# The two halves of a column group on rows of their own in the closing of a decode block: four vector operations over 64 columns and a store of 16 rows

## The chip, the cores and the metric

One core of one Trainium2 chip. The metric is device time in microseconds of one execution; lower is better. The span is the time from the first to the last instruction of one profiled execution, and all positions in the text (226.41 and the like) are microseconds from its start.

## What is computed

One decode step of a transformer block for two sequences (B = 2, one token each, D = 512), all in float32. Six modulation vectors come from `silu(c) @ w_mod`; then an attention over the last 4096 positions of a cache, then a feed-forward part, each gated:

```python
mod = (_silu(c) @ w_mod).reshape(c.shape[0], 6, 1, -1)
sa, ca, ga, sb, cb, gb = (mod[:, i] for i in range(6))
h = _layernorm(x) * (1 + ca) + sa
x = x + ga * attention(h, k_cache, v_cache, wq, wo)      # 32 heads, 8 key heads, last 4096 of 32768
h = _layernorm(x) * (1 + cb) + sb
x = x + gb * (_silu(h @ w1) @ w2)                          # w1 512 x 1792, w2 1792 x 512
```

The change is in the last line: the product with w2, the gate gb, the sum with x (called x1 in the kernel) and the store of the result, 2 x 512 numbers.

## The kernel before, in words

Nearly all of the time goes into reading weights and caches, 97.5 MB. Every load is issued by SyncE, in order, into a ring of eight slots of 16 KB a partition (`stream`, L70); a load starts when the slot's last reader is done. The order is w_mod, wq, eight pairs of key and value blocks, wo in two loads, w1 in two, and w2 in four: its 128-row tiles 0 to 7, 8 to 10, 11 and 12, and 13 (L599).

Two sequences fill only 2 of 128 partitions, so the kernel keeps a vector of 512 as four column groups of 128, and each group on its own 32 partitions: partition 32g + 16b holds columns 128g to 128g + 127 of sequence b. This is the layout of x1, of gb (a part of `mod_sp`) and of the result. Products use TensorE as four tiles side by side, each with weights of 128 x 32, whose column 16b holds sequence b; such a product fills the 32 rows of one group. A product in float32 is two instructions.

The tail, in order (names as in the trace):
- `busy(3)` (L641): products into `junk` whose result nobody reads.
- x1 is finished early, at L643, though it stands behind the junk products in the code. The hidden vector is turned, scaled and put through SiLU; `uT` (L657) holds it as 14 tiles of 128 x 32 weights, column 16b for sequence b.
- `yw` (L661): tiles 0 to 7 of w2, 512 columns each, spread over the four row groups; each row group so holds a part of the sum over all 512 columns.
- `y` (L671): tiles 8 to 10, one product of 128 columns for each column group g, into rows 32g.
- `gather` (L546): ScalarE and then VectorE copy the halves of yw to SBUF (L549, L550), and four products with `id4` (L552) add the four row groups up and put each column group on its rows, added to y.
- `yl` (L686): tiles 11 to 13, each column group in two halves of 64 columns, the halves in two banks of PSUM.
- The closing, on VectorE: y times gb (L694) plus x1 (L695), 128 columns each; then for each half, yl times gb (L699), and for each half the sum of both (L702).
- The store (L704): one DMA by SyncE, 8 rows of 128 numbers, from partitions 32g + 16b.

`inorder` keeps the instructions of one engine that are wrapped in it in the order of the code; the others are placed by the framework's scheduler where their data allow. The matmuls and the vector operations of the tail are wrapped, the copies by ScalarE and GpSimd's operations are not. `const` makes a tile for the whole kernel; tiles of one `tag` in the pool `once` share one place, and a new one waits for the last reader of the one before. Lines are those of the kernel before. The functions that the change touches:

Of the kernel before, what the change touches and what calls it, by code (L numbers as in the profile page):

```python
# [8 lines left out]
F32 = mybir.dt.float32  # L9
# [4 lines left out]
P = 128  # L14
B, D = 2, 512
# [8 lines left out]
def adaln_block(  # L24
# [19 lines left out]
    nc = tc.nc  # L44
# [7 lines left out]
    id4 = head.tile([P, 32], F32, name="id4")  # L52
    ring = ctx.enter_context(tc.tile_pool(name="ring", bufs=1))
    consts = ctx.enter_context(tc.tile_pool(name="consts", bufs=1))
    ktp = ctx.enter_context(tc.tile_pool(name="ktp", bufs=4))
    work = ctx.enter_context(tc.tile_pool(name="work", bufs=2))
    once = ctx.enter_context(tc.tile_pool(name="once", bufs=1))
# [3 lines left out]
    def const(shape, name):  # L61
        return consts.tile(shape, F32, name=name)

    def bank(tag, name):
        return (psum1 if tag in "CO" else psum).tile([P, 512], F32, tag=tag, name=name)
# [36 lines left out]
    rows8 = lambda t: t.rearrange("(ab r) m -> ab r m", r=16)[:, 0, :]  # L102
# [10 lines left out]
    ident = const([P, P], "ident")  # L113
# [98 lines left out]

    oTn = const([P, 32, 32], "oTn")
    nc.gpsimd.memset(oTn, 0.0)
    mod_a = const([P, 2, P], "mod_a")
    mod_sp = const([P, 4, P], "mod_sp")
    x1 = const([P, P], "x1")

    def silu_exp(t, name, shape):

        e = once.tile(shape, F32, tag="silu", name=name)
        nc.vector.tensor_scalar(e, t, -1.0, 87.0, op0=ALU.mult, op1=ALU.min)
        nc.scalar.activation(e, e, AF.Exp)
        nc.vector.tensor_scalar(e, e, 1.0, None, op0=ALU.add)
        nc.vector.reciprocal(e, e)
        return e
# [26 lines left out]
    def turned(t, name):  # L253
        o = const([P, 4, 32], name)
        nc.vector.transpose(o, t.rearrange("p (m k) -> p k m", k=4))  # L255
        return o
# [7 lines left out]
    for k in range(4):  # L264
        ab = wm[:, k, : 2 * D].rearrange("p (s g m) -> p g s m", s=2, g=4)
        cd = wm[:, k, 2 * D :].rearrange("p (s g m) -> p g s m", s=4, g=4)
        for g in range(4):
            r = slice(32 * g, 32 * g + 32)
            nc.tensor.matmul(m_a[r, :], scT[:, k, :], ab[:, g], start=(k == 0), stop=(k == 3))  # L269
        for g in range(4):  # L270
            r = slice(32 * g, 32 * g + 32)
# [11 lines left out]
    nc.vector.tensor_mul(h_a, xn, mod_a[:, 1, :])  # L283
    nc.vector.tensor_add(h_a, h_a, mod_a[:, 0, :])
    hq_T = turned(h_a, "hq_T")
    nc.scalar.copy(mod_sp.rearrange("p s m -> p (s m)"), m_sp)
    nc.gpsimd.tensor_scalar(mod_sp[:, 2, :], mod_sp[:, 2, :], 1.0, None, op0=ALU.add)
    ga, sb, cb1, gb = (mod_sp[:, s, :] for s in range(4))


    hT, uT = const([P, 4, 32], "hT_b"), const([P, F // P, 32], "uT")
    nc.gpsimd.memset(hT, 0.0)
    nc.gpsimd.memset(uT, 0.0)

    q_ps = [bank("D", f"q{n}") for n in range(2)]
    for n in range(2):
        for k in range(4):
            wv = wqt[:, k, :].rearrange("p (n s g m) -> p n g s m", n=2, s=4, g=G)  # L300
            for g in range(G):
# [4 lines left out]
                    start=(k == 0),  # L306
                    stop=(k == 3),
                )

    inorder = tc.keep_in_program_order  # L310
# [193 lines left out]
    ax = once.tile([P, P], F32, tag="ax", name="ax")  # L504
# [17 lines left out]
    for r in (0, 64):  # L522
# [4 lines left out]
            start=True,  # L527
            stop=True,
# [17 lines left out]
    def gather(acc, wide, name, start, stop):  # L546

        sb_ = once.tile([P, D], F32, tag="wide", name=name)
        nc.scalar.copy(sb_[:, : D // 2], wide[:, : D // 2])  # L549
        inorder(nc.vector.tensor_copy(sb_[:, D // 2 :], wide[:, D // 2 :]))  # L550
        for g in range(4):
            inorder(nc.tensor.matmul(  # L552
                acc[32 * g : 32 * g + 32, :],
                id4,
                sb_[:, g * P : (g + 1) * P],
                start=start,
                stop=stop,
            ))
# [15 lines left out]
    acc = bank("D", "acc_o")  # L574
    ao = bank("A", "ao")[:, :P]
    busy(6)
    for q in range(28):
        g = q % 4
# [4 lines left out]
            start=(q < 4),  # L583
            stop=(q >= 24),
        ))
    for q in range(28, 32):
        for g in range(4):
# [4 lines left out]
                start=(q == 28),  # L592
                stop=False,
# [3 lines left out]
    T2, WIDE = F // P, 8  # L597
    w2t = {}
# [26 lines left out]
    for k in range(4):  # L625
        for g in range(4):
# [4 lines left out]
                start=(k == 0),  # L631
                stop=(k == 3),
# [13 lines left out]
    z = once.tile([P, T2, B], F32, tag="z", name="z")  # L646
    for b in range(B):
        nc.vector.scalar_tensor_tensor(
            z[:, :, b],
            hidT[:, :, 16 * b],  # L650
            rstd[:, b : b + 1],
            hidT[:, :, 16 * b + 1],
            op0=ALU.mult,
            op1=ALU.add,
        )
    sg = silu_exp(z, "sgh", [P, T2, B])
    nc.vector.tensor_mul(uT[:, :, 0:32:16], z, sg)  # L657
    yw = bank("D", "acc_yw")
    for tt in range(WIDE):
        g = tt % 4  # L660
# [4 lines left out]
            start=(tt < 4),  # L665
            stop=(tt >= WIDE - 4),
        ))
    y = bank("D", "acc_y")[:, :P]
    for tt in range(WIDE, 11):
        for g in range(4):  # L670
            inorder(nc.tensor.matmul(  # L671
                y[32 * g : 32 * g + 32, :],
                uT[:, tt, :],
                w2t[tt][:, g * P : (g + 1) * P],
                start=(tt == WIDE),
                stop=False,
            ))
    gather(y, yw, "acc_y_sb", False, True)

    H = P // 2  # L680
    yl = [bank("A", f"acc_l{h}")[:, :H] for h in range(2)]
    for tt in range(11, T2):
        for h in range(2):
            for g in range(4):
                lo = g * P + h * H
                inorder(nc.tensor.matmul(  # L686
                    yl[h][32 * g : 32 * g + 32, :],
                    uT[:, tt, :],
                    w2t[tt][:, lo : lo + H],
                    start=(tt == 11),  # L690
                    stop=(tt == T2 - 1),
                ))
    yp = once.tile([P, P], F32, tag="xp", name="yp")
    inorder(nc.vector.tensor_mul(yp, y, gb))  # L694
    inorder(nc.vector.tensor_add(yp, yp, x1))  # L695
    yo = once.tile([P, P], F32, tag="yo", name="yo")
    for h in range(2):
        r = slice(h * H, (h + 1) * H)
        inorder(nc.vector.tensor_mul(yo[:, r], yl[h], gb[:, r]))  # L699
    for h in range(2):  # L700
        r = slice(h * H, (h + 1) * H)
        inorder(nc.vector.tensor_add(yo[:, r], yo[:, r], yp[:, r]))  # L702
    of = out.rearrange("b s d -> (b s) d")
    nc.sync.dma_start(of.rearrange("b (g m) -> g b m", m=P), rows8(yo))  # L704


_INS = ["A_x", "A_k_cache", "A_v_cache", "A_wq", "A_wo", "B_w1", "B_w2", "c", "w_mod"]
# [24 lines left out]
```

## Time and profile before

| | us |
|---|---|
| median of 3 runs | 235.51 |
| lowest and highest of them | 235.45, 235.78 |
| span of the profiled execution | 233.7 |
| TensorE, busy | 161.1 (69% of the span) |
| VectorE, busy | 115.6 (49%) |
| ScalarE, busy | 28.5 (12%) |
| GpSimd, busy | 10.5 (4%) |

Of the profiled execution the span is recorded, and no time of its own besides; the difference between the span and the lowest run, about 1.8 us, is what lies around it. An engine's busy time is an average over stages that wait for different things; for a change in the last 8 us, the rows of those 8 us decide.

### The profile page before, as it was taken

Reading aid. Unit: us, or ns where it says so; the run is one execution under the profiler, and the core shown is the slowest. Engines: PE = TensorE matmul, PEld = TensorE weight load, DVE = VectorE, ACT = ScalarE, POOL = GpSimd, SP = SyncE. Lnnn points to the kernel's source line nnn. Section 1 sums busy time; section 2 is a strip of 40 time slices with the busy share of each in tenths; the row PEclk is TensorE's granted clock in tenths of the full one; section 3 lists DMA queues with packets and bytes.
Section 4 is the critical chain, followed back from the end, with each engine's and each line's share of the span. In section 5 each row is a group of like instructions: output and inputs, shape, how many; then the busy total and the mean of one; then the engine's idle time right before and its main releaser. Section 6 shows DMA issues by size and latency. Waiting matters only on the chain.

```text
span 233.7 us, 2571 instructions
## 1 busy us (share of the span) xinstructions
PE 161.1 (69%) x1070; PEld 43.3 (19%) x1070; DVE 115.6 (49%) x179; ACT 28.5 (12%) x64; POOL 10.5 (4%) x35
## 2 busy tenths in 40 slices
PE   0004916859577839797598749759759779789684
PEld 0001401201111111211120201202112122324222
DVE  0007240278894758695197089259559540101232
ACT  2000210000311120120210201111020120102020
POOL 2004710000000000000000000000000000000000
PEclk9999985979999977999979999988997997999999
DMA  7998998999999999999999999999999999989991
GB/s 269 446 542 359 404 494 359 446 444 421 415 421 449 446 437 415 426 426 446 449 437 409 418 437 449 449 421 412 426 444 449 443 421 437 463 367 437 424 404 57
DMA packets 3794, 97.68 MB, mean 418 GB/s; under 512 B 432, under 2 KB 456, under 8 KB 968
## 3 DMA queue, kind: packets, MB, share of 16 engines
q1 hardware_dynamic: 3768, 97.53, 97.1%
q8 instruction: 8, 0.13, 0.2%
q14 instruction: 2, 0.02, 0.0%
q10 hardware_dynamic: 16, 0.00, 0.0%
HBM read 97.53 MB, written 0.00 MB: 417 GB/s over the span
## 4 chain that ended last, share of the span: by engine, by line
DMA 60%; issue 18%; DVE 14%; PE 6%; POOL 0%; SPq 0%; POOLq 0%; ACT 0%
DMA slots<-in_A_k_cache_dram 22%; DMA slots<-in_A_wq_dram 15%; DMA slots<-in_A_v_cache_dram 12%; DMA slots<-in_B_w_dram 12%; DVE kT L361 11%; PE o L448 2%; PE q L302 2%; DVE zp L420 1%; PE acc_yw L661 1%; DVE xp L418 1%; PE qr L323 0%; PE acc_y L671 0%; DVE qT L315 0%; POOL qg L319 0%; SPq L109 0%
## 5 line engine op out<-in xcount | busy, mean ns | idle before, releaser
L361 DVE STREAM_TRANSPOSE kT<-slots 128x1024 f32<-128x1024 f32 x64 | 73.7, 1212 | 23.7 <-DMA slots<-in_A_k_cache_dram 23.6
L374 PE MATMUL s<-kT,qbd 128*32 128x512 f32 x256 | 68.6, 693 | 19.1 <-DVE kT L361 18.0
L448 PE MATMUL o<-slots,ptb 128*32 128x512 f32 x256 | 30.8, 624 | 2.1 <-DMA slots<-in_A_v_cache_dram 2.1
L374 PEld LDWEIGHTS s<-kT,qbd 128*32 128x32 f32 x256 | 9.6, 113 | 68.4 <-DVE kT L361 63.4
L269 PE MATMUL m_a<-slots,scT 128*32 128x256 f32 x32 | 4.4, 506 | 20.5 <-DVE scT L261 20.5
L302 PE MATMUL q<-slots,hq_T 128*32 128x512 f32 x64 | 8.3, 680 | 7.0 <-DMA slots<-in_A_wq_dram 7.0
L448 PEld LDWEIGHTS o<-slots,ptb 128*32 128x32 f32 x256 | 8.1, 114 | 17.9 <-issue 17.8
L404 ACT COPY bias<-bp 128x1 f32<-128x1 f32 x8 | 1.3, 159 | 77.0 <-PE bp L402 77.0
L384 DVE TENSOR_REDUCE mx<-s 128x1 f32<-128x512 f32 x8 | 5.5, 691 | 9.6 <-PE s L374 9.6
L565 PE MATMUL junk<-quad,id 128*32 128x512 f32 x22 | 10.2, 595 | 0.0
L420 DVE TENSOR_TENSOR zp<-xp,quarter 128x1024 f32<-128x1024 f32 x8 | 9.8, 1225 | 0.2
L435 ACT ACTIVATE ptb<-pT,odd 128x256 f32<-128x256 f32 x16 | 6.7, 472 | 25.6 <-PE pT L427 25.6
L255 DVE STREAM_TRANSPOSE cT<-xc 128x128 f32<-128x128 f32 x1 | 0.4, 401 | 16.7 <-DMA xc<-in_c_dram 16.7
L427 PE MATMUL pT<-zp,mix 128*32 128x256 f32 x64 | 5.7, 428 | 3.6 <-DVE zp L420 3.5
L458 ACT COPY ob<-o 128x512 f32<-128x512 f32 x8 | 4.7, 585 | 26.1 <-PE o L448 26.1
L272 PE MATMUL m_sp<-slots,scT 128*32 128x512 f32 x32 | 7.4, 738 | 0.0
L386 PE MATMUL mT<-ident,mx 128*1 128x128 f32 x16 | 3.0, 270 | 6.3 <-DVE mx L384 6.3
L315 DVE STREAM_TRANSPOSE qT<-q 128x512 f32<-128x512 f32 x2 | 1.4, 717 | 11.7 <-PE q L302 10.2
L418 DVE STREAM_TRANSPOSE xp<-pr 128x512 f32<-128x512 f32 x8 | 5.5, 686 | 3.4 <-ACT pr L406 3.4
L579 PE MATMUL acc_o<-slots,oTn 128*32 128x512 f32 x56 | 6.2, 593 | 0.7 <-DMA slots<-in_A_wo_dram 0.7
L466 PE MATMUL o_all<-ob,selh 128*64 128x128 f32 x64 | 6.0, 316 | 0.8 <-ACT ob L458 0.8
L550 DVE COPY acc_o_sb<-acc_o 128x256 f32<-128x256 f32 x1 | 0.4, 425 | 12.4 <-ACT acc_o_sb L549 12.4
(140 smaller groups left out, 93.8 us busy)
## 6 DMA issues: line engine op xcount, KB each, us to landing
slots<-in_A_k_cache_dram SPq DMA_DIRECT2D x8, 4096.0 KB, 27.4
slots<-in_A_v_cache_dram SPq DMA_DIRECT2D x8, 4096.0 KB, 27.6
slots<-in_w_mod_dram SPq DMA_DIRECT2D x1, 6144.0 KB, 17.1
slots<-in_A_wo_dram SPq DMA_DIRECT2D x1, 6144.0 KB
slots<-in_B_w_dram SPq DMA_DIRECT2D x1, 2688.0 KB
slots<-in_A_wo_dram SPq DMA_DIRECT2D x1, 2048.0 KB, 29.5
slots<-in_B_w_dram SPq DMA_DIRECT2D x1, 2048.0 KB
slots<-in_B_w_dram SPq DMA_DIRECT2D x1, 896.0 KB
```

The source lines that it names most:

```text
L272: nc.tensor.matmul(m_sp[r, :], scT[:, k, :], cd[:, g], start=(k == 0), stop=(k == 3))
L302: nc.tensor.matmul(q_ps[n][32 * g : 32 * g + 32, :], hq_T[:, k, :], wv[:, n, g], start=(k == 0), stop=(k == 3),)
L361: inorder(nc.vector.transpose(kT[s, j][:, 32 * c : 32 * c + 32, :], kt[s].rearrange("p (n j r) -> p j n r", j=4, r=32)[:, j, 32 * c : 32 * ...
L374: inorder(nc.tensor.matmul(s_ps[s][r : r + 32, :], qbd[h // 4][:, h % 4, b, j, :], kT[s, j][:, 32 * c : 32 * c + 32, e:32:2], start=(j == ...
L418: inorder(nc.vector.transpose(xp, pr[s]))
L420: inorder(nc.vector.tensor_mul(zp, xp[:, None, :, 0:16].to_broadcast([P, 4, 16, 16]), quarter[:, :, None, None].to_broadcast([P, 4, 16, 16 ...
L427: inorder(nc.tensor.matmul(tp[32 * i : 32 * i + 32, :], mix.rearrange("p v e -> p (v e)"), zp.rearrange("p y t x -> p (y t) x")[:, :, 4 * ...
L435: inorder(nc.scalar.activation(ptb[s % 2][:, :, e, :], tp.rearrange("p (w z) -> p w z", z=16), AF.Copy, scale=odd[:, e : e + 1],))
L448: inorder(nc.tensor.matmul(o_ps[s][r : r + 32, :], ptb[s % 2][:, w].rearrange("p e z -> p (e z)"), vt[s].rearrange("p (c w m f d) -> p c f ...
L466: inorder(nc.tensor.matmul(o_all[r : r + 64, :], selh[:, m, lo : lo + 2 * HQ], o_sb[s][:, m * DH : (m + 1) * DH], start=(s == 0 and m < 2) ...
L565: inorder(nc.tensor.matmul(junk[0:32, :], id4, quad.rearrange("p m y -> p (m y)"), start=True, stop=True,))
L579: inorder(nc.tensor.matmul(acc[32 * g : 32 * g + 32, :], oTn[:, q, :], wot[q], start=(q < 4), stop=(q >= 24),))
```

## The change

The column group of 128 is split in halves h of 64, and half h of group g goes to partition 32g + 16h + 8b, so that all vector work of the closing has 64 columns on twice as many rows. For this the weights get columns at 16h + 8b:
- `uL` (in the place of `zp`, cleared by GpSimd) holds tiles 8 to 13 of uT twice, once for each h; ScalarE copies them from uT. `halves` makes eight products of 64 columns for one tile (two h, four g), all into one bank.
- `idh` is id4 with its columns at 16h + 8b, made by GpSimd near the start; the gather becomes `halves` with idh, eight products of 64 columns instead of four of 128.
- gb and x1 must lie on the same rows. `shift` (in the place of `mod_a`, made by GpSimd when mod_a has been read) is a pair of full 128 x 128 weights that move a half to its rows; four products into `gxp`, in order behind the junk products and ahead of yw, and a copy by ScalarE give `gx`: gb and x1 with 64 columns each.
- yl is one bank instead of two; the closing is four operations instead of six; the store has 16 rows of 64 numbers instead of 8 of 128.

```diff
+    idh = const([P, 2, 32], "idh")
+    nc.gpsimd.memset(idh, 0.0)
+    for h in range(2):
+        nc.gpsimd.tensor_copy(idh[:, h, 16 * h : 16 * h + 16 : 8], id4[:, 0:32:16])
...
+    shift = consts.tile([P, 2, 4, 32], F32, tag="mod_a", name="shift")
+    nc.gpsimd.memset(shift, 0.0)
+    for h in range(2):
+        nc.gpsimd.tensor_copy(
+            shift[:, h, :, 16 * h : 16 * h + 16 : 8],
+            ident.rearrange("p (g r) -> p g r", g=4)[:, :, 0:32:16],
+        )
...
+    uL = once.tile([P, 2, T2 - WIDE, 32], F32, tag="zp", name="uL")
+    nc.gpsimd.memset(uL, 0.0)
     sg = silu_exp(z, "sgh", [P, T2, B])
     nc.vector.tensor_mul(uT[:, :, 0:32:16], z, sg)
+    for h in range(2):
+        nc.scalar.copy(uL[:, h, :, 16 * h : 16 * h + 16 : 8], uT[:, WIDE:, 0:32:16])
+    def halves(acc, weights, moving, start, stop):
+        for h in range(2):
+            for g in range(4):
+                lo = g * P + h * H
+                inorder(nc.tensor.matmul(
+                    acc[32 * g : 32 * g + 32, :],
+                    weights(h),
+                    moving[:, lo : lo + H],
+                    start=start and h == 0,
+                    stop=stop and h == 1,
+                ))
+    gxp = bank("C", "gx")[:, : 2 * H]
+    for i, t in enumerate((gb, x1)):
+        for h in range(2):
+            inorder(nc.tensor.matmul(
+                gxp[:, i * H : (i + 1) * H],
+                shift[:, h].rearrange("p g r -> p (g r)"),
+                t[:, h * H : (h + 1) * H],
+                start=(h == 0),
+                stop=(h == 1),
+            ))
+    gx = once.tile([P, 2, H], F32, tag="ax", name="gx")
+    nc.scalar.copy(gx, gxp)
...
-    y = bank("D", "acc_y")[:, :P]
+    y = bank("D", "acc_y")[:, :H]
+    yl = bank("A", "acc_l")[:, :H]
     for tt in range(WIDE, 11):
...
+        halves(y, lambda h: uL[:, h, tt - WIDE, :], w2t[tt], tt == WIDE, False)
-    gather(y, yw, "acc_y_sb", False, True)
+    ys = once.tile([P, D], F32, tag="wide", name="acc_y_sb")
+    nc.scalar.copy(ys[:, : D // 2], yw[:, : D // 2])
+    inorder(nc.vector.tensor_copy(ys[:, D // 2 :], yw[:, D // 2 :]))
+    halves(y, lambda h: idh[:, h, :], ys, False, True)
     for tt in range(11, T2):
...
+        halves(yl, lambda h: uL[:, h, tt - WIDE, :], w2t[tt], tt == 11, tt == T2 - 1)
-    yp = once.tile([P, P], F32, tag="xp", name="yp")
-    inorder(nc.vector.tensor_mul(yp, y, gb))
-    inorder(nc.vector.tensor_add(yp, yp, x1))
-    yo = once.tile([P, P], F32, tag="yo", name="yo")
-    for h in range(2):
-        r = slice(h * H, (h + 1) * H)
-        inorder(nc.vector.tensor_mul(yo[:, r], yl[h], gb[:, r]))
-    for h in range(2):
-        r = slice(h * H, (h + 1) * H)
-        inorder(nc.vector.tensor_add(yo[:, r], yo[:, r], yp[:, r]))
+    yp = once.tile([P, H], F32, tag="xp", name="yp")
+    inorder(nc.vector.tensor_mul(yp, y, gx[:, 0, :]))
+    inorder(nc.vector.tensor_add(yp, yp, gx[:, 1, :]))
+    yo = once.tile([P, H], F32, tag="yo", name="yo")
+    inorder(nc.vector.tensor_mul(yo, yl, gx[:, 0, :]))
+    inorder(nc.vector.tensor_add(yo, yo, yp))
-    nc.sync.dma_start(of.rearrange("b (g m) -> g b m", m=P), rows8(yo))
+    nc.sync.dma_start(
+        of.rearrange("b (z m) -> z b m", m=H),
+        yo.rearrange("(zb r) m -> zb r m", r=8)[:, 0, :],
+    )
```

More of the change, by code (lines that the diff above doesn't have):

```diff
@@ L214, in adaln_block @@
     nc.gpsimd.memset(oTn, 0.0)
-    mod_a = const([P, 2, P], "mod_a")
+    idh = const([P, 2, 32], "idh")
+    nc.gpsimd.memset(idh, 0.0)
+    for h in range(2):
+        nc.gpsimd.tensor_copy(idh[:, h, 16 * h : 16 * h + 16 : 8], id4[:, 0:32:16])
+    mod_a = consts.tile([P, 2, P], F32, tag="mod_a", name="mod_a")
     mod_sp = const([P, 4, P], "mod_sp")
@@ L293, in adaln_block @@
     nc.gpsimd.memset(uT, 0.0)
+    H = P // 2
     q_ps = [bank("D", f"q{n}") for n in range(2)]
@@ L667, in adaln_block @@
         ))
-    y = bank("D", "acc_y")[:, :P]
+    y = bank("D", "acc_y")[:, :H]
+    yl = bank("A", "acc_l")[:, :H]
     for tt in range(WIDE, 11):
[L670 to L677, printed above, removed]
-    gather(y, yw, "acc_y_sb", False, True)
-    H = P // 2
-    yl = [bank("A", f"acc_l{h}")[:, :H] for h in range(2)]
@@ L682, in adaln_block @@
-    for tt in range(11, T2):
-        for h in range(2):
[L684 to L692, printed above, removed]
-    yp = once.tile([P, P], F32, tag="xp", name="yp")
-    inorder(nc.vector.tensor_mul(yp, y, gb))
@@ L695, in adaln_block @@
-    inorder(nc.vector.tensor_add(yp, yp, x1))
-    yo = once.tile([P, P], F32, tag="yo", name="yo")
-    for h in range(2):
-        r = slice(h * H, (h + 1) * H)
-        inorder(nc.vector.tensor_mul(yo[:, r], yl[h], gb[:, r]))
-    for h in range(2):
-        r = slice(h * H, (h + 1) * H)
-        inorder(nc.vector.tensor_add(yo[:, r], yo[:, r], yp[:, r]))
+        halves(y, lambda h: uL[:, h, tt - WIDE, :], w2t[tt], tt == WIDE, False)
+    ys = once.tile([P, D], F32, tag="wide", name="acc_y_sb")
```

## The prediction

> **What bounds the kernel now.** First the page: its slices say whether loads or engines set the pace.
>
> ```profile
> span 233.7 us, 2571 instructions
> DMA  7998998999999999999999999999999999989991
> q1 hardware_dynamic: 3768, 97.53, 97.1%
> ```
>
> The DMA queue that carries all loads is at work for 97.1% of the span and falls away only in the last slice. So the loads set when the tail may begin, and an engine counts only after the last piece that it waited for. The chain of waits, in order of time, shows where that is.
>
> ```profile
> 198.74 27.57 DMA slots<-in_B_w_dram
> 226.30 0.14 issue
> 226.44 1.92 PE acc_yw L661 x16
> ```
>
> At 226.30 the first eight tiles of w2 land; from there the rest of the chain is products and vector operations: compute sets the end. All that the change does behind 226.30 counts in full, and what ends before counts nothing. Now the timeline of the tail (start, length, engine, line, in brackets the wait before it).
>
> ```profile
> 216.17 0.29 DVE L643 TENSOR_TENSOR x<-xc,ax 128x128 f32<-128x128 f32 x1
> ...
> 222.94 2.74 PE L565 MATMUL junk<-quad,id 128*32 128x512 f32 x6
> 225.36 0.21 DVE L657 TENSOR_TENSOR uT<-z,sgh 128x28 f32<-128x28 f32 x1
> 226.41 0.19 PEld L661 LDWEIGHTS acc_yw<-slots,uT 128*32 128x32 f32 x8 [1.64 <-DVE uT L657]
> 226.44 1.92 PE L661 MATMUL acc_yw<-slots,uT 128*32 128x512 f32 x16 [0.76 <-DMA slots<-in_B_w_dram]
> 228.28 0.86 PE L671 MATMUL acc_y<-slots,uT 128*32 128x128 f32 x24
> 228.47 0.37 ACT L549 COPY acc_y_sb<-acc_yw 128x256 f32<-128x256 f32 x1 [3.73 <-PE acc_yw L661]
> 228.88 0.42 DVE L550 COPY acc_y_sb<-acc_yw 128x256 f32<-128x256 f32 x1 [3.32 <-ACT acc_y_sb L549]
> 229.36 0.14 PEld L552 LDWEIGHTS acc_y<-acc_y_sb,id 128*32 128x32 f32 x4 [0.28 <-DVE acc_y_sb L550]
> 229.48 0.25 PE L686 MATMUL acc_l<-slots,uT 128*32 128x64 f32 x2
> 229.53 0.93 PE L686 MATMUL acc_l<-slots,uT 128*32 128x64 f32 x46
> 229.82 0.29 DVE L694 TENSOR_TENSOR yp<-acc_y,mod_sp 128x128 f32<-128x128 f32 x1 [0.51 <-PE acc_y L552]
> 230.14 0.29 DVE L695 TENSOR_TENSOR yp<-yp,x 128x128 f32<-128x128 f32 x1
> 230.42 0.36 DVE L699 TENSOR_TENSOR yo<-acc_l,mod_sp 128x64 f32<-128x64 f32 x2
> 230.70 0.35 DVE L702 TENSOR_TENSOR yo<-yo,yp 128x64 f32<-128x64 f32 x2
> 231.07 0.64 SPq L704 DMA_DIRECT2D out_dram<-yo  x1
> ```
>
> Three things are to be seen. TensorE is free from the last junk product (modelled end 222.94 + 2.74 = 225.68) to 226.41: a gap of 0.73 us ahead of the yw products. From 229.82 VectorE works without a pause to 231.05 (1.23 us), and that ends the chain. But TensorE ends the yl products (L686) at 230.46, only 0.04 us after VectorE begins to read them: both are nearly bound there.
>
> **The change part by part.** I count in the profiled execution: span 233.7, about 1.8 us less than the median of 235.51 (lowest run 235.45); this difference, work outside the span, is carried over unchanged.
>
> *Constants and early copies* (idh, shift, uL's memset on GpSimd). No row shows them; the nearest are these.
>
> ```profile
> 27.40 0.20 POOL L292 MEMSET hT_b<- 128x128 f32 x1
> 31.05 0.53 POOL L287 TENSOR_SCALAR mod_sp<-mod_sp 128x128 f32<-128x128 f32 x1 [3.04 <-ACT mod_sp L286]
> 31.83 0.20 POOL L503 COPY hT_b<-sbT 128x8 f32<-128x8 f32 x1 [0.24 <-DVE sbT L255]
> 43.11 0.52 POOL L319 COPY qg<-qT 32x32 f32<-32x32 f32 x2 [11.08 <-DVE qT L315]
> ```
>
> idh: a memset (0.20) and two copies (0.20 each), 0.6 us in the 3.04 us that GpSimd waits before 31.05. shift: a memset of twice that width (at most 0.40) and two copies, 0.8 us; taking over mod_a's place it waits for the last read of mod_a (in the making of h_a, ahead of wq's products), and behind it queue L287 and L503, needed only late in the kernel, and then 11.08 us of waiting. uL's memset (three times the width, at most 0.6) can run when aoT has been read, at about the time of L643, and is needed at 225.6. All cost nothing; without that cover it would be some 2 us of GpSimd.
>
> *uL's copies on ScalarE.* Two copies of 128x12 between uT (225.57) and the first y product. The nearest row, a 128x28 activation, and the next work of ScalarE:
>
> ```profile
> 224.52 0.23 ACT L223 ACTIVATE sgh<-sgh 128x28 f32<-128x28 f32 x1 [1.44 <-DVE sgh L222]
> ```
>
> Two by 0.23 end near 226.1. Their readers begin after 228.28 and ScalarE's next work is at 228.47: nothing. Even with the gx copy queued ahead of them (below) they end near 227.6.
>
> *gxp*: four new products, gb and x1 moved to the new rows. They are full-array (128x128 weights) and stand in program order between the junk products and yw. x1 has been ready since 216.46 (L643), so they wait only for TensorE, and all of yw is queued behind them. The trace holds the same shape eight times, at L539, and the same change of shape behind narrow products at L636.
>
> ```profile
> 200.87 0.97 PEld L539 LDWEIGHTS oq<-on,quad 128*128 128x128 f32 x8 [1.02 <-PE o_all L466]
> 200.90 1.07 PE L539 MATMUL oq<-on,quad 128*128 128x64 f32 x8 [0.81 <-DVE on L536]
> 201.90 0.14 PEld L565 LDWEIGHTS junk<-quad,id 128*32 128x32 f32 x2
> ...
> 219.46 1.71 PE L627 MATMUL hid<-slots,hT_b 128*32 128x448 f32 x16 [1.30 <-DMA slots<-in_B_w_dram]
> ...
> 221.10 0.30 PEld L636 LDWEIGHTS var_b<-vs,mean 128*128 128x128 f32 x2 [0.73 <-issue]
> ```
>
> Eight instructions (two per product) hold TensorE from 200.87 until the next weights at 201.90: 1.03 us. The full-array weights at 221.10 did not come ahead of the narrow products; they came 0.07 before those products' modelled end (219.46 + 1.71 = 221.17). So gxp starts at 225.68 - 0.07 = 225.61 and yw's first weights at 225.61 + 1.03 = 226.64, where they were at 226.41: **+0.23**. The gap covers 0.80 of the 1.03. Lower bound 0, if gxp's weights load under the junk products; upper bound with the slower pace of L636 (0.30 for two, so 1.20 for eight) from 225.68: 226.88, +0.47. I take 0.23, the row of the same count and shape.
>
> The Trainium skill, "TensorEngine Tiling (Array Packing)", Key Properties, says that a change of tiling mode drains TensorE, and speaks against this change, which puts two such changes ahead of yw; L636's start 0.07 before the modelled end agrees. "TensorE: Matmul & The Clock Gate" (the Trainium skill), Step-by-step, says that the next weights can be pulled ahead while products run; by that rule gxp would begin earlier, and the term would fall toward its lower bound.
>
> gx's copy on ScalarE (128x128) begins near 226.7 and ends before 227.1; ScalarE's next work is the yw copy at 228.5. Nothing.
>
> *y, gather, yl on TensorE.* y goes from 24 instructions of 128 columns to 48 of 64, the gather from 8 of 128 to 16 of 64, yl stays at 48 of 64. The pace of a 64-wide one:
>
> ```profile
> L686 PE MATMUL acc_l<-slots,uT x48: 216/219/243, 229.5 to 230.2; 128*32 128x64 f32 x48
> ```
>
> The last starts at 229.53 + 0.93 - 0.22 = 230.24, so 47 steps from 229.48 take 0.76: 0.0162 each. y takes 48 x 0.0162 = 0.78 from 228.28 to 229.06, and four of the gather to 229.13: still under VectorE's copy, which releases the gather's other half at 229.36. Behind that release stand now 12 gather instructions (0.19) where 4 took 0.12 to yl's start (229.36 to 229.48): yl begins and ends 0.09 later with its first weight load, at 230.55 instead of 230.46.
>
> *Closing vector operations.* Six become four, all 64 wide.
>
> ```profile
> L699 DVE TENSOR_TENSOR yo<-acc_l,mod_sp x2: 215/220/225, 230.4 to 230.6; 128x64 f32<-128x64 f32 x2
> ```
>
> Halving the columns saves 0.07 of the 0.29 of L694 and L695, no half. Also the pairs at L699 and L702 overlap today (two in 0.36), while the two new pairs are each dependent, which costs the length and 0.03 between (229.82 + 0.29 to 230.14). The gather's last end stays near 229.78, so yp runs from 229.83: multiply to 230.05, add 230.08 to 230.30. Then VectorE must wait: yl has one bank and is read whole, at 230.55 + 0.05 = 230.60. Multiply to 230.82, add 230.85 to 231.07, store at 231.09 against 231.07: **+0.02**. The cover is gone: today one half's additions and multiplications hide the last yl products. Lower bound, with yl in time: multiply at 230.30, store at 230.79, -0.28. Upper bound, if the 12 gather instructions keep the 0.03 that the four show (0.36 for 0.19): +0.19.
>
> *Store*: 16 rows of 256 bytes for 8 of 512. Nearest issues by rows:
>
> ```profile
> L105 ACTq DMA_DIRECT2D xc<-in_c_dram x4: 485/488/1076, 1.2 to 3.3; - x4
> L109 SPq DMA_DIRECT2D xc<-in_A_x_dram x1: 701/701/701, 1.2 to 1.2; - x1
> 92.88 0.53 SPq L82 DMA_DIRECT2D slots<-in_A_k_cache_dram  x1
> ```
>
> Two rows take 0.49 and eight 0.70, 0.036 a row, but a load of 128 partitions takes 0.53: rows alone do not set it. Below, 0.53 against the 0.64 of L704: -0.1. Above, eight rows by 0.036: +0.28. I take 0, nearer to the large load, which has by far the most rows.
>
> **Sum**: 0.23 + 0.02 + 0 = +0.25, so span 233.95 and time 235.51 + 0.25 = **235.76**. A difference under 0.2%, 0.47 us, is about what a measurement of this kernel can't tell from no change.
>
> **The rivals.**
> *gxp hides and the closing gains* (faster side): weights come under the junk products, so yw keeps 226.41, and yl comes in time. -0.28: 235.23; with half of it, 235.4. For it: 0.73 us of gap, and an yl pace that may differ in one bank. Against: L636, and 60 instructions behind the release.
> *The store pays by row* (slower side): descriptors are written one by one, and from 0.036 a row the store's issue adds 0.28: +0.53, 236.04. It decides from 0.22 on (0.25 + 0.22 = 0.47). For it: L105 against L109. Against: the 0.53 of the large load.
> *Short rows are read before they are written*: from the issue's end (231.71) to the span's end are 1.99 us; a second trip of half that adds 1.0: 236.76. No store of short rows is in this trace to speak for or against it. The Trainium skill, "DMA: Bandwidth & Descriptors", Specifications, says that below 512 bytes a read-modify-write happens; no run here shows it yet.
> *It doesn't do what it says*: the operations get no shorter by width. With 0.29 for 0.22 at the two behind yl, 0.14 more: 235.90. Against: L699.
>
> **How the numbers follow.** Forecast 0.47, gxp hidden 0.20, store by row 0.19, read before write 0.06, no shorter operations 0.05, others 0.03. Only the best case with a shorter store passes -0.47: faster 0.04. Slower: the two store cases and a part of the upper bounds (gxp's +0.47 and the closing's +0.19 give 0.66 without the store), 0.28. Same: 0.68. The range reaches from the hidden case, 235.2, to the store by row with a little of gxp's upper bound, 236.25.
>
> **What would show it.** In the changed profile: first yw weights near 226.64 with the wait before them put on gxp, not on the load (else the first term is wrong); yw copy near 228.7; a pause of VectorE of some 0.3 us between yp's add and the yo multiply, ended by acc_l; four operations of 0.22; the store's issue near 231.3 and 0.64 long; 2.0 us from its end to the span's end. If the load of w2 lands later than 226.6, gxp hides and the +0.23 is not seen.

## The result, and the profile after

| | before | after |
|---|---|---|
| median of 20 runs | 235.59 | 236.87 |
| lowest and highest | 235.26, 236.15 | 235.59, 237.96 |
| median span | 233.7 | 234.85 |
| time outside the span, median | 1.72 to 1.81 by session | 1.98 |

The ratio is 1.0046, 95% interval 1.0031 to 1.006: slower, by 1.28 us where 0.25 was forecast. The second thing to see is the scatter: 20 spans of the changed kernel lie between 233.6 and 235.6, eight of them at 234.2 or less and twelve at 234.6 or more, where most spans of the kernel before (taken beside the experiments below) lie between 233.5 and 233.9. So one profile can't stand for the changed kernel. The first that was taken is one of the long ones. Its page:

```profile
span 235.3 us, 2660 instructions
...
q1 hardware_dynamic: 3780, 97.53, 96.5%
```

The loads still fill the span. The timeline of its tail, to be held against the one of before:

```profile
219.38 2.99 PE L639 MATMUL hid<-slots,hT_b 128*32 128x448 f32 x16 [1.04 <-DMA slots<-in_B_w_dram]
...
222.82 1.81 PE L639 MATMUL hid<-slots,hT_b 128*32 128x448 f32 x16
...
224.46 2.74 PE L577 MATMUL junk<-quad,id 128*32 128x512 f32 x6
...
227.13 0.52 PEld L691 LDWEIGHTS gx<-mod_sp,shift 128*128 128x128 f32 x4 [0.84 <-issue]
...
228.16 0.16 PEld L703 LDWEIGHTS acc_yw<-slots,uT 128*32 128x32 f32 x8
...
228.43 0.33 ACT L673 COPY uL<-uT 128x12 f32<-128x12 f32 x2
...
231.09 0.36 PE L680 MATMUL acc_y<-acc_y_sb,idh 128*32 128x64 f32 x10 [0.15 <-DVE acc_y_sb L716]
...
231.32 0.86 PE L680 MATMUL acc_l<-slots,uL 128*32 128x64 f32 x46
231.56 0.22 DVE L721 TENSOR_TENSOR yp<-acc_y,gx 128x64 f32<-128x64 f32 x1 [0.52 <-PE acc_y L680]
231.82 0.22 DVE L722 TENSOR_TENSOR yp<-yp,gx 128x64 f32<-128x64 f32 x1
232.23 0.22 DVE L724 TENSOR_TENSOR yo<-acc_l,gx 128x64 f32<-128x64 f32 x1 [0.19 <-PE acc_l L680]
232.49 0.23 DVE L725 TENSOR_TENSOR yo<-yo,yp 128x64 f32<-128x64 f32 x1
232.74 0.70 SPq L727 DMA_DIRECT2D out_dram<-yo  x1
```

From gxp on, each step is what was forecast: its weights start 0.07 before junk's modelled end (224.46 + 2.74 = 227.20), yw's first weights follow 1.03 later, VectorE pauses (232.04 to 232.23) until yl is there, four operations take 0.22 or 0.23. But all of it lies 1.5 us late, and that came earlier: the first 16 of the 32 instructions of hid (the products with w1) took 2.99, where before they took 1.71. The view by stretches (PE, PEld, DVE, ACT and POOL busy with counts, granted clock, DMA share, GB/s) says why:

```profile
216.20:219.60 3.40, 1.81 (x9) 0.62 (x12) 1.27 (x9) 0.00 (x0) 0.42 (x1) 1.00 0.99 422
219.60:223.00 3.40, 3.40 (x22) 1.23 (x18) 0.00 (x0) 0.07 (x1) 0.00 (x0) 0.51 1.02 436
```

The granted clock was 0.51 for one stretch of 3.4 us in which hid's products stood. (The Trainium skill, "TensorE: Matmul & The Clock Gate", What's actually happening, says that the clock falls to half after an idle window of about 3.4 us, and that these windows run freely. The length of the stretch and its clock agree; but in the 3.40 us ahead of it TensorE was busy for 1.81, so that stretch was not idle.) In the kernel before such a drop in hid would have met the 0.73 us ahead of yw, and one ahead of hid also the 1.30 us of waiting for w1; with gxp the 0.73 is used up. So the first theory was **lost cover**: gxp alone costs 0.25 in most executions, and every clock drop shows in full. The rivals were the time outside the span (store or number of instructions) and, once a trace showed it, the supply of instructions.

### The profile page after: what moved, and what is told of

The parts are those of the page before. It is cut to its first block, busy times and chain, and to the rows that moved or that the text cites. A ratio compares the mean times of both kernels' runs of the same rounds, so it can differ in the third digit from the quotient of the medians.

```text
span 235.3 us, 2660 instructions
## 1 busy us (share of the span) xinstructions
PE 163.5 (69%) x1110; PEld 44.6 (19%) x1110; DVE 115.3 (49%) x177; ACT 29.0 (12%) x67; POOL 11.8 (5%) x42
## 4 chain that ended last, share of the span: by engine, by line
DMA 61%; PE 18%; DVE 16%; ACT 1%; ACTq 1%; issue 1%; DVEq 0%
DMA slots<-in_A_k_cache_dram 42%; DMA slots<-in_B_w_dram 12%; DVE kT L373 12%; PE s L386 7%; DMA xc<-in_c_dram 6%; PE hid L639 2%; PE m_sp L276 2%; DVE zp L432 2%; PE o L460 2%; PE m_a L273 1%; PE junk L577 1%; ACTq L105 1%; DVE xp L430 1%; PE acc_yw L703 1%; DVE mx L396 1%
## 5 line engine op out<-in xcount | busy, mean ns | idle before, releaser
L386 PE MATMUL s<-kT,qbd 128*32 128x512 f32 x256 | 69.8, 713 | 17.4 <-DVE kT L373 16.4
L460 PE MATMUL o<-slots,ptb 128*32 128x512 f32 x256 | 29.1, 595 | 2.4 <-DMA slots<-in_A_v_cache_dram 2.4
L314 PE MATMUL q<-slots,hq_T 128*32 128x512 f32 x64 | 9.5, 759 | 7.5 <-DMA slots<-in_A_wq_dram 7.5
L276 PE MATMUL m_sp<-slots,scT 128*32 128x512 f32 x32 | 6.9, 722 | 0.0
```

The source lines that it names most:

```text
L276: nc.tensor.matmul(m_sp[r, :], scT[:, k, :], cd[:, g], start=(k == 0), stop=(k == 3))
L314: nc.tensor.matmul(q_ps[n][32 * g : 32 * g + 32, :], hq_T[:, k, :], wv[:, n, g], start=(k == 0), stop=(k == 3),)
L386: inorder(nc.tensor.matmul(s_ps[s][r : r + 32, :], qbd[h // 4][:, h % 4, b, j, :], kT[s, j][:, 32 * c : 32 * c + 32, e:32:2], start=(j == ...
L460: inorder(nc.tensor.matmul(o_ps[s][r : r + 32, :], ptb[s % 2][:, w].rearrange("p e z -> p (e z)"), vt[s].rearrange("p (c w m f d) -> p c f ...
```

## The experiments

Ratios are to runs of the kernel before on the same chip; spans are of all runs. An expectation speaks of the theories as they stood when it was written: theory A is lost cover, theory B says that another part of the change makes the clock drop, and theory C, the supply of instructions, first shows in the sixth kernel. The expectations number the kernels in the order of their runs: e1 has gxp alone, e3 has gxp ahead of hid, e6 is the kept-busy one, e9 the changed one with 108 instructions more.

**gxp alone, and all but gxp.** To the kernel before, only shift, the four products and their copy are added, with nobody reading gx:

```diff
+    shift = consts.tile([P, 2, 4, 32], F32, tag="mod_a", name="shift")
...
+    gxp = bank("C", "gx")[:, : 2 * H]
...
+    gx = once.tile([P, 2, H], F32, tag="ax", name="gx")
+    nc.scalar.copy(gx, gxp)
     yw = bank("D", "acc_yw")
```

> The kernel before with nothing of the change but shift, the four gxp products between the junk products and yw, and the copy to gx, which nobody reads. Theory A (cover): the hidden products run at half clock in over half of the executions, with the change and without it; before, the free 0.73 us ahead of yw took up most of that loss of 1.28 us, and gxp has used this gap up. Then this kernel alone shows the result: +0.2 us in executions at full clock, +1.0 to 1.2 us in those with the drop, median +0.7 to +1.1. Theory B (drop): another part of the change, such as GpSimd's clearing of uL at 216.5 or the 64-column products, makes the clock drop, which the kernel before never does there: +0.23 us in all executions.

Measured: 235.91, ratio 1.0017 (1.0003 to 1.0031); six spans at 233.7 to 234.0, five at 234.3 to 234.5, one at 235.7. In the changed kernel the products are left out instead, so that its gate and sum use rows that are not moved:

```diff
-    gxp = bank("C", "gx")[:, : 2 * H]
...
-    nc.scalar.copy(gx, gxp)
+    for i, t in enumerate((gb, x1)):
+        nc.scalar.copy(gx[:, i, :], t[:, :H])
```

> The changed kernel without the gxp products: ScalarE copies the first 64 columns of gb and x1 in their place, so the gate and the sum of the closing use rows that are not moved. Theory A: the gap ahead of yw is back, so the median is that of before, -0.2 to +0.1 us, and the spread that of before. Theory B: the clock still drops in over half of the executions, median +0.4 us or more over before.

Measured: 235.77, ratio 1.0012 (1.0003 to 1.002); spans 233.5 to 233.9, as before, and yw waits for the load again:

```profile
226.27 1.92 PE L694 MATMUL acc_yw<-slots,uT 128*32 128x512 f32 x16 [0.77 <-DMA slots<-in_B_w_dram]
```

The parts don't add up: gxp alone costs 0.4, the rest without gxp 0.27, the whole 1.28. Something arises only where both are there.

**The cover given back.** If lost cover is the cause, gxp ahead of hid, where TensorE waits for w1, must cure it; and one more junk product ahead of hid, against the clock drop, must narrow the scatter.

```diff
     busy(1)
+    nc.vector.tensor_mul(ax, ao, ga)
+    nc.vector.tensor_add(x1, x_sp, ax)
+    gxp = bank("C", "gx")[:, : 2 * H]
...
+    nc.scalar.copy(gx, gxp)
     FC = F // 4
```

> The changed kernel with the same four gxp products, but in TensorE's order behind the junk product that follows the mean and ahead of the hidden products, where TensorE waits some 1.0 to 1.3 us for w1. Theory A: gxp is then free and the gap ahead of yw is whole again: median -0.3 to +0.1 us. Theory B, if the drop does not come from gxp: +0.4 us or more; if it comes from the idle time ahead of the hidden products, which gxp now fills, -0.2 us as well.

```diff
-    busy(1)
+    busy(2)
```

> The changed kernel with one more junk product behind the mean, 0.86 us of work in the idle time ahead of the hidden products. Both theories put the loss on the clock in the hidden products. If the drop comes from little work in the few microseconds ahead of them, it goes, and all executions lie where the fast ones of the change lie, +0.1 to +0.3 us. If the clock drops for another reason, over half stay at +1.2 to +1.5 us.

Measured: 236.47, 1.0046 (1.0029 to 1.0064), spans 233.6 to 235.6; and 236.83, 1.0048 (1.0032 to 1.0064), six spans at 233.8 to 234.6 and six at 235.2 to 235.4. Neither helps: lost cover is not the main cause. Next, the changed kernel once more, unedited, and one with junk products in each idle stretch of TensorE from 191 us on:

> The changed kernel once more, on the same chip as the next three. Theory A (cover), as it stands now: TensorE's clock falls to half for one window of some 3.4 us at places that differ from execution to execution, with or without the change; in the products with wo that costs 1.7 us, in the hidden products 1.3 us; before, 1.3 us of waiting for w1 and 0.73 us ahead of yw absorb it, and gxp has taken the second. Spans in groups: 233.7 to 234.0 without a drop, near 234.4 (drop in the wo products: 1.7 less 1.3, plus 0.23) and near 235.2 (drop in the hidden products: 1.3 plus 0.23). Theory B: the drop comes with the change and nearly all late executions are of one kind.

```diff
+        if s == STEPS:
+            junk2 = bank("C", "junk2")
+            for _ in range(2):
...
-    busy(6)
+    busy(8)
...
-    busy(1)
+    busy(2)
```

> The changed kernel with junk products in each idle stretch of TensorE from 191 us on: two ahead of the last value products, two more ahead of the wo products, one more ahead of the hidden products. gxp, the closing and the store are unchanged. Theory A: without idle stretches the clock does not fall, the late executions go, all spans within 0.4 us and near 233.8 to 234.2, median 235.8 to 236.1. If the late executions have another cause than the clock behind idle stretches, spans near 235 stay, in a third or more of the executions.

Measured: 237.05 (six runs), 1.0062 (1.0042 to 1.0082); and 236.22 (seven), 1.0045 (1.0026 to 1.0063), spans still 234.0 to 235.6. In the first, and in the kernel with gxp ahead of hid, the profiled execution shows another drop, in the products with wo (7.91 us, where the changed kernel's page has 6.2). The second, with no drop between 134 us and its last product and yet 235.6, held the answer. Its timeline:

```profile
229.86 0.63 PE L686 MATMUL acc_l<-slots,uL 128*32 128x64 f32 x31
...
232.04 0.43 PE L686 MATMUL acc_l<-slots,uL 128*32 128x64 f32 x15 [1.55 <-issue]
232.04 0.26 PEld L686 LDWEIGHTS acc_l<-slots,uL 128*32 128x32 f32 x14 [1.68 <-issue]
232.53 0.22 DVE L730 TENSOR_TENSOR yo<-acc_l,gx 128x64 f32<-128x64 f32 x1 [1.96 <-PE acc_l L686]
```

TensorE stands still in the midst of the yl products, with 33 of 48 done (31, and 2 in a row of their own), for nothing that the profile shows. (From here on the instructions are counted, of which a float32 product is two, each with its weight load.) The row's 1.55 counts from the modelled end of the product before. From start to start it is 1.77: the last of the 31 starts at 229.86 + 0.63 - 0.22 = 230.27, the next product at 232.04, where 0.016 is the usual step. In the trace a packet of the instruction queue (16384 bytes) runs from 229.32 to 230.55. That made the **block theory**: TensorE's list comes in blocks, and the change adds 80 TensorE instructions. The pages of before and after count its products and its weight loads:

```profile
PE 161.1 (69%) x1070; PEld 43.3 (19%) x1070; DVE 115.6 (49%) x179; ACT 28.5 (12%) x64; POOL 10.5 (4%) x35
```

```profile
PE 163.5 (69%) x1110; PEld 44.6 (19%) x1110; DVE 115.3 (49%) x177; ACT 29.0 (12%) x67; POOL 11.8 (5%) x42
```

So the border of a block comes to lie inside the yl products, whereas in the kernel before the list ends ahead of it.

**The rival outside the span.** The kernel before with 16 short rows stored (two DMAs, by SyncE and ScalarE), and with 19 tiny products ahead of `busy(6)`, so 76 instructions more, all read by nobody:

```diff
-    nc.sync.dma_start(of.rearrange("b (g m) -> g b m", m=P), rows8(yo))
+    for b, eng in ((0, nc.sync), (1, nc.scalar)):
+        eng.dma_start(
+            of[b].rearrange("(g h m) -> g h m", g=4, h=2),
+            yo.rearrange("(g q) h m -> g q h m", g=4)[:, 16 * b, :, :H],
+        )
```

> The kernel before with its result stored as 16 rows of 256 bytes, in two DMAs of 8 rows on two queues at once; the halves lie 32 bytes apart in the tile, nothing else is changed. The time outside the span was 1.74 us in the kernel before and in e1 (store of 8 rows) and 1.92 to 1.99 in all kernels with 16 rows, with some executions at 2.3 to 3.0. If short rows are the cause, it is 1.95 or more here, with such executions, and the median +0.2 to +0.4 us. If the number of instructions is the cause, 1.74 and a median within 0.1 us.

```diff
+    tiny = bank("C", "tiny")
+    for _ in range(19):
+        inorder(nc.tensor.matmul(tiny[0:32, 0:2], id4, quad[:, 0, 0:2], start=True, stop=True))
     busy(6)
```

> The kernel before with 19 products of 2 columns ahead of the junk products (76 instructions more, about as many as the change adds), into a bank that nobody reads, some 0.5 us in a stretch where TensorE only burns time. If the number of instructions sets the time outside the span: 1.95 us instead of 1.74, median +0.2 us. If not: 1.74, median within 0.1 us of the kernel before.

Measured: 235.77, 1.0013 (1.0004 to 1.0021), spans 233.8 to 234.2, outside 1.79; and 235.80, 1.0017 (1.0008 to 1.0025), spans 233.6 to 234.2, outside 1.83. Neither has the long spans. (Their median span is 234.0 for 233.7. In the first's profile the tail is that of before up to the store, and from the end of the issues, 231.77, to the span's end are 2.30 us, for 1.99. In the second's the clock was at half from 200.6 to 207.4, and hid began 1.0 late.) The second carries nearly as many TensorE instructions as the changed kernel, so their number alone isn't it. But its additions stand far ahead of the tail, and the eighth packet of the queue runs from 223.40 to 224.34, ahead of the tail, where in the kernel before it begins at 229.44, in the midst of it.

**The border moved.** 27 products of two columns (108 instructions) at three of the block pairs, far from the tail, in the changed kernel, in the kept-busy one, and in the one with gxp ahead of hid:

```diff
+        if s in (3, 4, 5):
+            tiny = bank("B", f"tiny{s}")
+            for _ in range(9):
+                inorder(nc.tensor.matmul(tiny[0:32, 0:2], id4, quad[:, 0, 0:2], start=True, stop=True))
```

> The changed kernel, tail untouched, with 27 products of 2 columns (108 instructions) in the middle of the kernel, where TensorE waits for keys. Theory C (instructions): TensorE's instructions come in blocks of 16 KB, one transfer for some 256 instructions; the change lengthens TensorE's list so that the last block begins inside yl (in e6 TensorE stopped there for 1.55 us at full clock, 33 of 48 instructions in, while the block's transfer had run between 229 and 231), and its transfer waits behind w2. 108 instructions more put that border ahead of the tail and the next one behind the end: spans of 235 and more go, median span 233.8 to 234.3 as against 234.9, median time 235.8 to 236.2. Theory A (a lost cover for the clock) alone: over a third of the executions stay near 235.2.

> The same 108 instructions in the kernel of e6, whose idle stretches are filled with junk products. Theory C with the clock as the second cause: neither stop nor drop is left, spans 233.8 to 234.4 in all executions. If e6's late executions had to do with the added junk products and not with the border of a block, they stay near 235.5.

> The same 108 instructions in the kernel of e3, which has gxp ahead of the hidden products. Theory C: spans of 235 and more go; what is left is the clock in the wo products with the waiting for w1 used up by gxp, near 234.4 in a part of the executions; the others near 233.6, 0.1 under the kernel before, since gxp then costs nothing. Theory A alone: no change against e3.

| kernel | without the 108 | with them | spans with them |
|---|---|---|---|
| changed | 1.0046 (1.0031 to 1.006) | 1.0018 (1.0009 to 1.0026) | 233.7 to 234.3 |
| kept busy | 1.0045 (1.0026 to 1.0063) | 1.0018 (1.0007 to 1.0028) | 233.7 to 234.5 |
| gxp ahead of hid | 1.0046 (1.0029 to 1.0064) | 1.0012 (1.0002 to 1.0023) | 233.5 to 234.6 |

More instructions make the kernel faster: by the medians 0.77, 0.22 (where the intervals touch) and 0.72 us, and the spans over 234.6 are gone. (Two more kernels with the 108 instructions follow below; there one execution each is long, 235.7 and 235.3, and was not profiled. Of all five, two of 54 executions lie over 234.6, where eleven of the changed kernel's 20 did.) The timeline of the changed kernel with them:

```profile
226.82 1.92 PE L707 MATMUL acc_yw<-slots,uT 128*32 128x512 f32 x16
...
229.75 0.36 PE L684 MATMUL acc_y<-acc_y_sb,idh 128*32 128x64 f32 x10 [0.15 <-DVE acc_y_sb L720]
...
229.97 0.87 PE L684 MATMUL acc_l<-slots,uL 128*32 128x64 f32 x46
...
231.40 0.70 SPq L731 DMA_DIRECT2D out_dram<-yo  x1
```

The 46 yl products run in 0.87 without a gap. Of the instruction queue's packets one now runs at 218.32, and the next begins at 230.17. With gxp ahead of hid as well, yw waits for its load again:

```profile
226.33 1.92 PE L707 MATMUL acc_yw<-slots,uT 128*32 128x512 f32 x16 [0.73 <-DMA slots<-in_B_w_dram]
```

**The stop in the changed kernel itself** was still to be seen. Two more executions of it:

> The changed kernel, one profile. Theory C: if its span is 234.8 or more with the clock at full speed from the wo products on, TensorE stops inside yl for 0.7 to 1.6 us some 10 instructions before the end, and the last instruction block's transfer ran at 229 or later. With a span of 234.3 or less there is no such stop. Theory A: a late execution shows a clock drop in the wo or the hidden products.

> The same once more: a stop inside yl in a late execution at full clock, none in an early one (theory C); a clock drop in every late one (theory A).

The first has a span of 235.0. Its timeline and the end of its chain of waits:

```profile
226.67 1.92 PE L703 MATMUL acc_yw<-slots,uT 128*32 128x512 f32 x16
...
229.82 0.78 PE L680 MATMUL acc_l<-slots,uL 128*32 128x64 f32 x41
...
230.32 0.23 DVE L722 TENSOR_TENSOR yp<-yp,gx 128x64 f32<-128x64 f32 x1
...
231.57 0.31 PE L680 MATMUL acc_l<-slots,uL 128*32 128x64 f32 x5 [0.97 <-issue]
231.93 0.22 DVE L724 TENSOR_TENSOR yo<-acc_l,gx 128x64 f32<-128x64 f32 x1 [1.38 <-PE acc_l L680]
```

```profile
230.02 0.58 PE acc_l L680 x41
230.59 0.97 issue
231.57 0.33 PE acc_l L680 x5
```

hid ran at full clock, yw began where forecast (226.67 for 226.64), and what the span lost beyond that is the stop, 5 of 48 before the end: from start to start 229.82 + 0.78 - 0.22 = 230.38 to 231.57, 1.19 us. The second has a span of 234.0 and a stop at the same place, of 0.15 by its row and 0.37 from start to start (230.14 to 230.51):

```profile
229.59 0.77 PE L680 MATMUL acc_l<-slots,uL 128*32 128x64 f32 x41
...
230.51 0.31 PE L680 MATMUL acc_l<-slots,uL 128*32 128x64 f32 x5 [0.15 <-issue]
230.52 0.14 PEld L680 LDWEIGHTS acc_l<-slots,uL 128*32 128x32 f32 x4 [0.28 <-issue]
```

Now what the DMA queues moved, in 228.0 to 229.3 and then in 229.3 to 230.4 of the first, and in 228.0 to 229.3 of the second (packets, MB, share):

```profile
q1 hardware_dynamic: 114, 0.27, 52.5%
```

```profile
q1 hardware_dynamic: 16, 0.02, 5.9%
q8 instruction: 1, 0.02, 5.2%
```

```profile
q1 hardware_dynamic: 120, 0.28, 54.2%
q8 instruction: 1, 0.02, 4.4%
```

In the trace the packet runs from 229.39 to 230.31 in the first and from 228.15 to 229.07 in the second. The loads moved as much in 228.0 to 229.3 in both, so why the packet began within that stretch in one and behind it in the other stays open. The products go on at 231.57 and 230.51, 1.26 and 1.44 behind its end (1.49 in the kept-busy kernel). In the profile shown at the top it ended at 229.02 and yl came late, so nothing stopped.

The place goes by the count of instructions and not by time: behind the border stand 5 products and 4 weight loads, 9, in the changed kernel, and 15 and 14, 29, in the kept-busy one, which has 5 junk products of two instructions and two weight loads each more: 20. So in all three stopped profiles 2211 products and weight loads are done (2220 - 9 and 2240 - 29). The pages of the kernels that don't stop fit this, if the last packet ahead of a border is the one that brings its block:
- Before has 2140, gxp alone 2156, the changed kernel without gxp 2204: their lists end ahead of the border.
- The kernel with 19 tiny products has 2216, so the border lies 5 before its end, but its packet was there 6 us earlier.
- The changed kernel with the 108 has 2328, so the border lies 117 before its end, in the gather, some 10 us behind the packet at 218.32. So the tail still holds a border; its block is there in time.

(The Trainium skill, "Runtime: NRT & Kernel Launch", Instruction fetch mechanics, says that instruction memory is refilled in blocks of 16 KiB, 256 instructions, by the sequencer's own queue, and that crossing a border is mostly hidden. Packets of 16384 bytes and the counted place agree; mostly hidden does not hold at this border, which cost up to 1.19 us in the changed kernel. What the earlier borders cost, no run here shows.)

**The 0.2 outside the span.** Three kernels: the changed one with the 108 instructions and two stores of 8 short rows (SyncE, ScalarE); the kernel before with idh, uL and uL's two copies alone, read by nobody; the changed one with the 108 instructions and a store of 8 rows of 512 bytes, half of it zeros, so that half of the result is left out.

```diff
+    for q, eng in ((0, nc.sync), (1, nc.scalar)):
+        eng.dma_start(
+            of.rearrange("b (z m) -> z b m", m=H)[4 * q : 4 * q + 4],
+            yo.rearrange("(zb r) m -> zb r m", r=8)[8 * q : 8 * q + 8, 0, :],
+        )
```

> As e9, with the 16 rows stored by two DMAs of 8 rows on two queues. It asks where the 0.22 us outside the span come from (1.74 us with 8 rows, 1.95 with 16 rows in one DMA, 1.79 with 16 short rows in two DMAs of the kernel before). If the single DMA of 16 rows makes them, about 1.79 here. If the layout or the number of instructions makes them, about 1.95.

```diff
+    idh = const([P, 2, 32], "idh")
+    nc.gpsimd.memset(idh, 0.0)
...
+    uL = once.tile([P, 2, T2 - WIDE, 32], F32, tag="zp", name="uL")
+    nc.gpsimd.memset(uL, 0.0)
...
+        nc.scalar.copy(uL[:, h, :, 16 * h : 16 * h + 16 : 8], uT[:, WIDE:, 0:32:16])
```

> The kernel before with idh, uL's clearing and ScalarE's two copies into uL, none of which anybody reads. If the new constants and copies make the 0.22 us outside the span: 1.95 us, median +0.2 us. If not: 1.74, median within 0.1 us.

```diff
+    yof = once.tile([P, P], F32, tag="yo", name="yo")
+    nc.gpsimd.memset(yof[:, H:], 0.0)
+    yo = yof[:, :H]
...
+    nc.sync.dma_start(of.rearrange("b (g m) -> g b m", m=P), rows8(yof))
```

> As e9, but the result is taken from 8 rows of 128 numbers, of which 64 are zeros and half of the rows left out, so that the store has the old shape (8 rows of 512 bytes) behind the new closing. If the store of 16 rows makes the 0.22 us outside the span: 1.74 to 1.8 us, and a median 0.2 us under e9's (near 235.85). If the rest of the tail makes it: 1.95, median near 236.1.

Measured, in this order: 236.03, 1.0029 (1.0016 to 1.0043), outside 1.94; 235.80, 1.0011 (1.0002 to 1.002), spans 233.6 to 233.9 and one of 234.4, outside 2.04; 235.99, 1.0027 (1.0013 to 1.0042), outside 2.10. So neither two stores nor a store of long rows brings the 0.2 back, and the constants with their copies suffice for it, with the store of before. With gxp alone it is 1.71. But with the 19 tiny products, which have no such constants, five of eleven executions have 1.99 to 2.21, where the kernel before never has more than 1.89. So what this time goes by is open: nothing in the span shows it.

No kernel beat the one before; the best of the changed ones, gxp ahead of hid with the 108 instructions, has 1.0012.

## Why the prediction was wrong, point by point

- **The step that failed: "yl begins and ends 0.09 later with its first weight load, at 230.55".** The pace of 0.0162 was read from yl products with no border among them and applied to a list that is 80 instructions longer; the supply of instructions was no term. In its place the runs showed a stop inside yl that cost 0.37 us where the block's packet began at 228.15 and 1.19 where it began at 229.39 (0.15 and 0.97 by the rows, which count from a modelled end). Moving the border took the median span from 234.85 to 234.0: about 0.85 of the 1.28. That the packet is late because w2's loads fill the queues was only argued, and the windows above don't bear it out: as many load packets ran beside the early one. How many of the long executions have the stop and how many a clock drop isn't known either; of the three that were profiled, two have the stop, and the one shown at the top has the drop.
- **The second that failed: "work outside the span, is carried over unchanged".** It grew by about 0.2. Constants that cost nothing in the span suffice for that; the mechanism is open.
- **Clock drops** were no term either. Four of the profiles with the change show one in the products with wo or in hid. That they count more once the 0.73 ahead of yw is spent would explain why five of twelve spans with gxp alone stand 0.5 above the rest; this was argued and not tried by itself. It is the smaller part of the loss in the median, since the border's 0.85 and the 0.2 outside leave 0.23, about what was forecast.
- **gxp, +0.23: right**, to the hundredth, wherever it was profiled: 0.07 ahead of junk's modelled end and 1.03 long. With gxp alone the median is 0.41 up, for the six longer spans. The rival that it hides was wrong, and so is its time.
- **Constants, early copies and uL's copies cost nothing: right within the span** (233.8 in the median with them alone, for 233.7).
- **The closing, +0.02: nearly.** From the gather's second release to the store's issue, before took 229.36 to 231.07, 1.71; with the border moved 229.75 to 231.40, 1.65: -0.06. yl ends 1.09 behind the release, where it was 1.10: twelve gather instructions cost 0.17 before yl starts, where four cost 0.12, and yl itself takes 0.92, where it took 0.98 (that its one bank makes this was not tried by itself). VectorE's pause is 0.19, where some 0.3 was expected.
- **The store, 0: right.** Its issue takes 0.70 for 0.64, and from the issue's end to the span's end 235.3 - 233.44 = 1.9, for 1.99: neither a price by row as large as 0.28, nor a second trip. (Two such stores at once, in the kernel before, have 2.30 there.)
- With the border moved the median is 236.10: the span's +0.3 is the forecast's +0.25, and the 0.2 outside comes on top.

## What to carry to other kernels

A small edit can cost through its length: count the instructions that it adds to an engine, and look for the packets of the instruction queue near the end, where the list may now run into a block that is not there yet; an idle time put down to "issue" in the midst of equal products is the mark. If undoing either of two parts heals most of the loss, the parts don't have prices of their own, and something they share (here the length of a list) should be looked for. Profile more than one execution when spans scatter: the first profile here showed another cause, true of that execution, that was the smaller part of the loss.

## What the runs showed of the hardware that was not expected

- A block's packet took 0.92 us (1.23 in the kept-busy kernel), and TensorE goes on 1.26 to 1.49 us behind its end. Where the packet had ended longer ago, nothing stopped: at 229.02 for a border at 231.85 in the first profile, at 224.34 for one in the yl products that ran from 229.93 with the 19 tiny products.
- At 0.0162 us from one 64-wide product with its weights to the next, yl with its 48 is through in 0.9 us, so a packet that begins when yl does, and is of use 0.92 + 1.26 = 2.2 us later, comes too late for a border inside it.
- Eight full-array instructions between narrow products held TensorE for 1.03 or 1.04 us in each of the eleven profiles that have them ahead of yw.
- Time outside the span is no constant: the medians are 1.71 to 1.83 for kernels with the old tail, 1.93 to 2.10 for the changed tail and for the constants alone, and single executions reach 3.0.
